# A spectral layer and a gated feed-forward: two subtractions go from GpSimd to VectorE, and their products are reordered

## The chip, the cores and the metric

The kernel runs on one core of one Trainium2 chip. The metric is the device time of one execution in microseconds (us). A core has TensorE (PE, the matrix unit; PEld is its weight load), VectorE (DVE), ScalarE (ACT), GpSimd (POOL) and SyncE (SP), which issues the DMAs here. Each engine works through its own list of instructions in order, and semaphores make one engine wait for another.

## The reference

```python
N, D, F = 8192, 448, 1792            # tokens, channels, hidden width
def _A_ref(x, w1, b1, w2, b2):       # Fourier mixing over the tokens
    Xf = rfft2(x, axes=(1, 2))
    ...                              # two complex block layers, ReLU between, soft threshold
    return irfft2(Yf, (H, W), axes=(1, 2))
def _B_ref(x, w_gate, w_up, w_down):
    return (_gelu(x @ w_gate) * (x @ w_up)) @ w_down
mod = (_silu(c) @ w_mod).reshape(1, 6, 1, -1)      # sa, ca, ga, sb, cb, gb
h = _layernorm(x) * (1 + ca) + sa
x = x + ga * _A_ref(h, A_w1, A_b1, A_w2, A_b2)
h = _layernorm(x) * (1 + cb) + sb
x = x + gb * _B_ref(h, B_w_gate, B_w_up, B_w_down)
```

## The kernel before

The first 390 us or so make the transform, the block layers and the first half of the inverse transform, whose result `vd` goes to memory. The rest works on 32 chunks of 256 tokens (`CB` = 2 tiles of 128). For a chunk it multiplies `vd` by the inverse matrix `g` (`inverse` or `winverse`), adds the residual, normalizes, and runs the feed-forward, whose hidden width is cut into 7 units (`NP`). Numbers are kept to near fp32 by splitting each into a high and a low part: `gh` and `gl` of the matrix, `vh` and `vl` of the data. `split` makes a high part by a copy on ScalarE (L115) and the low part by a subtraction on the engine given as `el` (L117). An inverse then takes three products for each tile: `gh vh`, `gl vh`, `gh vl`.

Chunks 0 to 7 (`NSTD` = 8) are the standard stage, about 390 to 775 us. For each, `gate_up` runs 14 groups k = 0 to 13 of gate and up matmuls, and after k = 2 `down` multiplies the chunk before by the down weights. `down` is a fast 2x2 scheme with seven products of 21 matmuls each (L1313 to L1315: high by high, high by low, low by high). The products share few PSUM banks: the fifth needs the one that held the third, and ScalarE's copy at L1346 empties it. Between the products, `down` calls `mid(0)`, `mid(1)` and `mid(2)`, at which other work is put into the engines' lists.

That other work is, in chunks 1 to 7, the making of the weights' *forms* for the later stage: sums and differences of gate and up weight blocks of one unit (`form_sums` parts 0, 1 and 2, at L1683, L1685 and L1688 to L1690), their cast to fp16 on ScalarE (`forms_hi`, L1719) and the low parts on VectorE (`forms_lo`, L1727). The lists `start` (chunk 1) and `steady` (chunks 2 to 7) set where each step stands. In `steady`, part 1 stands at k = 2, the form cast that reads its result (number 4) at `mid(0)`, right ahead of L1346 on ScalarE. GpSimd's list there also holds the low parts of the inverse for the chunk two ahead (`split_g`, `split_v`, put in at k = 1).

Chunks 8 to 31 are the wide stage, about 775 us to the end. It runs `period(u)` for each of 168 units: `stage_a(u)` (32 matmuls at L1496), `stage_d(u-2)` (12), `stage_c(u-1)` (22), `stage_b(u)` (10). Between stages c and d of a unit, VectorE's `joins` (L1533, L1539) read what c left in PSUM. Then come the two gelu parts on ScalarE (L1545, L1553), their multiplications on VectorE (L1549, L1556), four sums on GpSimd (L1289 to L1292), and quantization (ScalarE L1561, VectorE L1571). Once in 7 periods, at k = 2, `phase` runs `winverse` for the chunk two ahead (L1620 to L1622), its residual (L1150) and `down` of the chunk before. That chunk's data are split at k = 0 (`split_v`: ScalarE L1120, GpSimd L1123 in four pieces) and its matrix at k = 1 (`split_g`), behind that period's other work.

Of the kernel before, what the change touches and what calls it, by code (L numbers as in the profile page):

```python
# [16 lines left out]
ALU = mybir.AluOpType  # L17
# [23 lines left out]
NSTD = 8  # L41
# [9 lines left out]
def spectral_geglu(ctx, tc, x, w1, b1, w2, b2, wg, wu, wd, cvec, wmod, cf1, cs2, cmi, cgm, out):  # L51
    nc = tc.nc
    V, S, G, T = nc.vector, nc.scalar, nc.gpsimd, nc.tensor
# [59 lines left out]
    def split(hi, lo, src, eh=None, el=None):  # L113

        (eh or S.copy)(hi, src)  # L115
        h = hi.bitcast(F32) if hi.dtype == F32R else hi
        (el or V).tensor_tensor(lo, src, h, ALU.subtract)  # L117
# [26 lines left out]
    with ExitStack() as actx:  # L144
# [227 lines left out]
        pe, start = 0.0, {}  # L372
# [36 lines left out]
    with ExitStack() as bctx:  # L409
# [576 lines left out]
        draws, nxt, x1t = {}, {}, {}  # L986
# [60 lines left out]
        def split_g(i):  # L1047
            gh = ep.tile([128, CB, 128], F32R, tag="gh", name="gh")
            gl = ep.tile([128, CB, 128], F32R, tag="gl", name="gl")
            split(gh, gl, nxt[i]["g"], el=G)  # L1050
            nxt[i]["g"] = gh, gl

        def down_hi(t):
# [38 lines left out]
    with ExitStack() as cctx:  # L1092
# [523 lines left out]
        def winverse(i, ps2):  # L1616
            nxt[i]["ps"] = [ps2[:, b, 0:D] for b in range(CB)]
            (gh, gl), vh, vl = nxt[i]["g"], nxt[i]["vh"], nxt[i]["vl"]
            for b, ps in enumerate(nxt[i]["ps"]):
                T.matmul(ps, gh[:, b], vh[:, b], start=True, stop=False)  # L1620
                T.matmul(ps, gl[:, b], vh[:, b], start=False, stop=False)
                T.matmul(ps, gh[:, b], vl[:, b], start=False, stop=True)  # L1622

        def down_banks(pf):
            return lambda q: (pdn[0], pdn[1], pf[:, 0, :], pdn[0], pf[:, 1, :], pdn[1], pdn[0])[q]
# [1 line left out]
        def phase(i):  # L1627

            u = i * NP + LA
            pf = sets[(u + 1) % 3]  # L1630
            j = i + 2
            on(u - 3, quant_lo)
            if j < nch:
                winverse(j, pf)
                residual(j)
            steps = {
                0: [(stats2,), (rsqrt_part, 5)],
                1: [(rsqrt_part, 9), (norm2, 0)],
                2: [(norm2, 1)],
            }  # L1640

            def mid(n):
                for fn, *args in steps[n] if j < nch else []:
                    fn(j, *args)

            down(i - 1, down_banks(pf), mid)

        extra = {
            0: [(2, split_v)],
            1: [(2, split_g), (1, wtransposes, [0])],  # L1650
            2: [(1, wtransposes, range(1, 5))],
            3: [(2, token_sums, 0), (2, wpack_hi, [0, 1]), (2, wpack_lo, [0, 1])],
# [26 lines left out]
        def form_sums(t, part):  # L1679
            r = raws[("w", t)]  # L1680
            a11, a12, a21, a22 = (r[:, q, h : h + 3].rearrange("p c x -> p (c x)") for q in range(2) for h in (0, 3))
            if part == 0:
                G.tensor_tensor(a21, a21, a22, ALU.add)  # L1683
            elif part == 1:
                G.tensor_tensor(a11, a21, a11, ALU.subtract)  # L1685
            else:
                e1, e2 = r[:, 0, 6], r[:, 1, 6]
                G.tensor_tensor(e1, e2, e1, ALU.subtract)  # L1688
                G.tensor_tensor(a12, a12, a11, ALU.subtract)
                G.tensor_tensor(a11, a22, a11, ALU.subtract)  # L1690
# [48 lines left out]
        def store_forms(t, part):  # L1739
# [5 lines left out]
        start = [  # L1745
            (0, load_forms),
            ("m0", form_sums, 0),
            ("m0", forms_hi, 0),
            ("m1", forms_lo, 0),
            ("m1", forms_hi, 2),  # L1750
            ("m2", forms_lo, 2),
            ("m2", form_sums, 1),
            ("m2", forms_hi, 1, 3),
            (3, forms_lo, 1, 3),
            (3, forms_hi, 4),
            (4, forms_lo, 4),
            (4, form_sums, 2),
            (4, forms_hi, 5),
            (5, forms_lo, 5),
# [38 lines left out]
        for n, k in enumerate((4, 7, 11, 13)):  # L1798
# [3 lines left out]
        hooks = {  # L1802
            5: [(1, turn)],
            1: [(2, split_g), (2, split_v)],
            6: [(2, inverse)],
            7: [(2, residual)],
# [8 lines left out]
        def later_by_one(k):  # L1815
# [14 lines left out]
        soon = {  # L1830
            0: [(1, token_sums, 0), (1, token_sums, 1), (1, wpack_hi, range(3)), (1, wpack_lo, range(3))],
            1: [(1, wpack_hi, [3, 4]), (1, wpack_lo, [3, 4]), (2, split_g), (2, split_v)],
            5: [(1, turn)],
            6: [(2, inverse)],
# [137 lines left out]
        for u in range(U0, NT_ + 1):  # L1972
            period(u)
            i, k = divmod(u, NP)
# [99 lines left out]
```

## Time and profile before

| | us |
|---|---|
| median of 3 runs | 1879.49 (1878.55 to 1882.35) |
| the profiled execution | 1880.26 |
| its span, first to last instruction | 1878.5 |
| PE busy | 1818.6 (97%) |
| DVE busy | 1395.4 (74%) |
| ACT busy | 994.9 (53%) |
| POOL busy | 1330.9 (71%) |
| mean granted TensorE clock | 0.989 |

The profile is of one execution. A row of its timeline gives start and duration in us, engine, line of the kernel, operation, output <- inputs, shapes and count; a bracket gives the idle time before it and what ended that. A row of the waits says which engine and line waited for which, with the total, the number and the longest. Matrices in PSUM and SBUF carry the program's names: `pdn` are the banks of `down`, `set` the three bank sets of the wide stage, `ws` and `wr` the forms and the raw weights, `ac` the quantized activations.

### The profile page before, as it was taken

To read this page: it belongs to the slowest core of one execution; us is meant where nothing else is said; L and a number is where in the kernel's file an instruction comes from. 1 tells how busy PE (TensorE), PEld (TensorE's weight loads), DVE (VectorE), ACT (ScalarE), POOL (GpSimd) and SP (SyncE) were. 2 spreads that over 40 slices of the span, in tenths; PEclk is the share of its full clock that TensorE was granted. 3 is DMA by queue.
4 is the path that set the end of the run, shared out by engine and by line. 5 is a ranking of instruction groups with operands and counts; after the bars stand their busy time and mean duration, and the time that the engine had idled before them with its cause. 6 is when DMAs were issued, how large, how long until landed. Compare 5 with 4: busy or idle time off the path is not lost.

```text
span 1878.5 us, 55991 instructions
## 1 busy us (share of the span) xinstructions
PE 1818.6 (97%) x23040; PEld 1713.3 (91%) x23040; DVE 1395.4 (74%) x2916; ACT 994.9 (53%) x1924; POOL 1330.9 (71%) x1760
## 2 busy tenths in 40 slices
PE   7999999899999998999999999999999999999998
PEld 3698999788888887899999999999999999999998
DVE  8787999878566666777777777777777777777755
ACT  5676778544333334355555555555555555555443
POOL 3466888258677777677777777777777777777634
PEclk9999999999999999999999999999999999999999
DMA  9987778754444434966666667666666666766561
GB/s 352 332 273 248 245 197 230 209 102 103 103 104 103 89 77 102 287 175 172 178 186 174 182 181 183 175 170 170 171 170 170 175 182 176 176 183 179 151 181 56
DMA packets 386232, 332.02 MB, mean 177 GB/s; under 512 B 116404, under 2 KB 364344, under 8 KB 385976
## 3 DMA queue, kind: packets, MB, share of 16 engines
q1 hardware_dynamic: 385976, 328.45, 64.0%
q8 instruction: 180, 2.95, 0.7%
q14 instruction: 76, 0.62, 0.1%
HBM read 243.32 MB, written 60.10 MB: 162 GB/s over the span
## 4 chain that ended last, share of the span: by engine, by line
PE 41%; POOL 35%; DVE 9%; issue 6%; DMA 5%; ACT 2%; SPq 1%; POOLq 0%; ACTq 0%; DVEq 0%
POOL x L1290 6%; PE pdn L1313 5%; PE pdn L1315 5%; PE pdn L1314 5%; PE set L1496 4%; POOL x L1289 4%; PE pgu L1240 4%; POOL x L1292 4%; POOL pk L1467 3%; POOL v L1123 3%; POOL x L1328 3%; POOL cq L1327 3%; PE set L1313 2%; PE set L1315 2%; PE set L1314 2%
## 5 line engine op out<-in xcount | busy, mean ns | idle before, releaser
L1496 PE MATMUL set<-nt,wk 128*128 128x128 f16 x12768 | 717.8, 219 | 2.4 <-DMA wk<-wk 1.1
L1496 PEld LDWEIGHTS <-wk 128*128 128x128 f16 x12768 | 715.2, 98 | 2.9 <-issue 1.5
L1313 PE MATMUL pdn<-wd,ac 128*128 128x224 f16 x1218 | 318.9, 262 | 17.0 <-ACT cq L1346 17.0
L1315 PE MATMUL pdn<-wd,ac 128*128 128x224 f16 x1218 | 318.7, 262 | 0.6 <-DVE ac L1301 0.6
L1314 PE MATMUL pdn<-wd,ac 128*128 128x224 f16 x1218 | 318.7, 262 | 0.0
L1240 PE MATMUL pgu<-nt,wk 128*128 128x256 f16 (+1 forms) x2464 | 268.2, 273 | 4.6 <-DVE x L1281 4.6
L1240 PEld LDWEIGHTS <-wk 128*128 128x128 f16 (+1 forms) x2464 | 225.7, 98 | 45.8 <-issue 20.4
L1571 DVE SCALAR_TENSOR_TENSOR ac<-x,sa_act,ac 128x896 f16<-128x896 f32 x168 | 213.5, 1271 | 38.1 <-ACT ac L1561 38.1
L1289 POOL TENSOR_TENSOR x<-x 128x128 f32<-128x128 f32 x223 | 146.5, 657 | 109.2 <-DVE x L1281 61.0
L1545 ACT ACTIVATE gl<-c,dg 128x384 f32<-128x384 f32 x168 | 103.1, 613 | 216.8 <-DVE c L1539 211.8
L1290 POOL TENSOR_TENSOR x<-x 128x128 f32<-128x128 f32 x223 | 193.1, 866 | 17.5
L1561 ACT ACTIVATE ac<-x,sa_act 128x896 f16<-128x896 f32 x168 | 174.8, 1040 | 48.8 <-POOL x L1292 42.0
L1359 POOL TENSOR_TENSOR cq<-cq 128x224 f32<-128x224 f32 x32 | 21.1, 659 | 241.1 <-DVE cq L1358 241.1
L1314 PEld LDWEIGHTS <-ac 128*128 128x128 f16 x1568 | 154.7, 99 | 18.9 <-issue 18.0
L1291 POOL TENSOR_TENSOR x<-x 128x128 f32<-128x128 f32 x223 | 166.9, 748 | 0.0
L1313 PEld LDWEIGHTS <-ac 128*128 128x128 f16 x1568 | 154.7, 99 | 5.7 <-issue 4.8
L1549 DVE TENSOR_TENSOR x<-c,gl 128x384 f32<-128x384 f32 x168 | 142.9, 851 | 18.1 <-ACT gl L1545 17.1
L1315 PEld LDWEIGHTS <-ac 128*128 128x128 f16 x1568 | 154.7, 99 | 1.7 <-DVE ac L1301 0.8
L1533 DVE TENSOR_TENSOR c<-set,sb 128x512 f32<-128x512 f32 x168 | 115.3, 686 | 36.2 <-PE set L1496 34.7
L1276 ACT ACTIVATE gel<-pgu,dg 128x256 f32<-128x256 f32 x112 | 49.4, 470 | 158.7 <-PE pgu L1240 150.9
L117 POOL TENSOR_TENSOR yl<-y,yh 128x448 fp32r<-128x448 f32 x63 | 87.9, 1411 | 55.1 <-ACT yh L115 54.8
L556 DVE SCALAR_TENSOR_TENSOR y<-pm,lam,t 64x224 f32<-64x224 f32 x256 | 115.1, 449 | 10.5 <-ACT t L548 6.7
(345 smaller groups left out, 3795.4 us busy)
## 6 DMA issues: line engine op xcount, KB each, us to landing
wk<-wk SPq DMA_DIRECT2D x76, 1024.0 KB, 9.3
wk<-wk SPq DMA_DIRECT2D x76, 768.0 KB, 5.0
tr<-td SPq DMA_DIRECT2D x32, 448.0 KB, 4.7
vd<-us SPq DMA_DIRECT2D x64, 224.0 KB, 3.1
xx<-in_A_x SPq DMA_DIRECT2D x32, 448.0 KB, 4.2
v<-vd SPq DMA_DIRECT2D x63, 224.0 KB, 5.6
out<-x SPq DMA_DIRECT2D x31, 448.0 KB, 7.6
xt<-in_A_x SPq DMA_DIRECT2D x15, 896.0 KB, 14.9
```

The source lines that it names most:

```text
L1240: T.matmul(pgu[i, t, q][:, pr * H : (pr + 1) * H], ws[rows, n, w, tw], nts[i][rows, tn, :], start=start, stop=stop, skip_group_check=True,)
L1289: e.tensor_tensor(s1, a21, a22, ALU.add)
L1290: e.tensor_tensor(s2, s1, a11, ALU.subtract)
L1291: e.tensor_tensor(s3, a11, a21, ALU.subtract)
L1313: T.matmul(ps, ac[:, 0, ka], w[:, 0, kb], start=n == 0, stop=False)
L1314: T.matmul(ps, ac[:, 0, ka], w[:, 1, kb], start=False, stop=False)
L1315: T.matmul(ps, ac[:, 1, ka], w[:, 0, kb], start=False, stop=n == NP - 1)
L1496: T.matmul(ps2[:, pr, reg * 128 : reg * 128 + 128], slot[:, pr, hl, wt, :], nt[:, xt, :], start=start and j == 0, stop=j == len(terms) - 1 ...
L1533: V.tensor_tensor(c[:, :, 1:3, :], p[:, :, 0:256].rearrange("p g (r c) -> p g r c", r=2), b[:, :, 0:128].rearrange("p g (o c) -> p g o c", ...
L1549: V.tensor_tensor(xs[u][:, 1::3, :], cts.pop(u)[:, 1], gls.pop(u), ALU.mult)
L1561: S.activation(ac[:, 0], xs[u][:, 0:7], AF.Copy, scale=sa_act[:, t : t + 1])
L1571: V.scalar_tensor_tensor(ac[:, 1], xs.pop(u)[:, 0:7], sa_act[:, t : t + 1], ac[:, 0], op0=ALU.mult, op1=ALU.subtract)
```

## The change

The diff:

```diff
@@ split_g
-            split(gh, gl, nxt[i]["g"], el=G)
+            split(gh, gl, nxt[i]["g"], el=V if i > NSTD + 2 else G)
@@ winverse
                 T.matmul(ps, gh[:, b], vh[:, b], start=True, stop=False)
-                T.matmul(ps, gl[:, b], vh[:, b], start=False, stop=False)
-                T.matmul(ps, gh[:, b], vl[:, b], start=False, stop=True)
+                T.matmul(ps, gh[:, b], vl[:, b], start=False, stop=False)
+            for b, ps in enumerate(nxt[i]["ps"]):
+                T.matmul(ps, gl[:, b], vh[:, b], start=False, stop=True)
@@ form_sums
             elif part == 1:
-                G.tensor_tensor(a11, a21, a11, ALU.subtract)
+                V.tensor_tensor(a11, a21, a11, ALU.subtract)
```

`V` is VectorE and `G` GpSimd. The subtraction of part 1 is made by VectorE in all seven chunks 1 to 7. The low inverse matrix `gl` is made by VectorE for chunks 11 to 31 (`i > NSTD + 2`), 21 of them; chunk 10 and those before keep GpSimd. In all 22 calls of `winverse`, the two products with `gl` come last. Lines behind L1622 are one further down in the changed kernel: L1685 is L1686 there.

GpSimd in chunk 5, before: the forms' sum (L1683), one unit's four sums, the inverse's two low parts, and the forms' differences.

```order
L1683 TENSOR_TENSOR wr<-wr 128x384
L1289 TENSOR_TENSOR x_9274<-x_9274 128x128
L1290 TENSOR_TENSOR x_9274<-x_9274 128x128
L1291 TENSOR_TENSOR x_9274<-x_9274 128x128
L1292 TENSOR_TENSOR x_9274<-x_9274 128x128
L117 TENSOR_TENSOR gl<-g,gh 128x256
L117 TENSOR_TENSOR v<-v,vh 128x896
L1685 TENSOR_TENSOR wr<-wr 128x384
L1688 TENSOR_TENSOR wr<-wr 128x128
```

VectorE in the same place, now: the low parts of the first two forms, the subtraction, and then the first result of `down` and the third low part.

```order
L1728 SCALAR_TENSOR_TENSOR ws<-wr,sww,ws 128x3x128 x2
L1686 TENSOR_TENSOR wr<-wr 128x384
L1341 TENSOR_TENSOR cq_3433<-pdn,cq_3432 128x224
L1728 SCALAR_TENSOR_TENSOR ws<-wr,sww,ws 128x128
L1731 COPY ws<-ws 128x2x128
L1728 SCALAR_TENSOR_TENSOR ws<-wr,sww,ws 128x3x128
L1349 TENSOR_TENSOR cq_3432<-pdn,cq_3432 128x224
```

The difference has moved from behind the inverse's low parts on GpSimd to ahead of L1341 on VectorE.

VectorE ahead of the inverse of chunk 11 in the wide stage, now: the last multiplication of a unit, the low matrix, the next unit's joins, a quantization and the next multiplications.

```order
L1556 TENSOR_TENSOR x_12376<-set_11355,gl_12392 128x128
L117 TENSOR_TENSOR gl<-g,gh 128x256
L1533 TENSOR_TENSOR c<-set_11356,sb 128x2x256
L1539 TENSOR_TENSOR c<-set_11356,sb 128x2x128
L1571 SCALAR_TENSOR_TENSOR ac<-x_12273,sa_act,ac 128x896
L1549 TENSOR_TENSOR x_12479<-c,gl_12476 128x3x128
L1556 TENSOR_TENSOR x_12479<-set_11356,gl_12495 128x128
```

Before, L1533 stood right behind the first L1556, and the row with `gl<-g,gh` stood on GpSimd between two units' sums. (`gl` followed by a number is another tile, the gelu's output.)

TensorE at the inverse of the same chunk, as a difference:

```order
 L1620 MATMUL set_11356<-vh,gh 128x448
-L1621 MATMUL set_11356<-vh,gl 128x448
-L1622 MATMUL set_11356<-v,gh 128x448
+L1621 MATMUL set_11356<-v,gh 128x448
 L1620 MATMUL set_11356<-vh,gh 128x448
-L1621 MATMUL set_11356<-vh,gl 128x448
-L1622 MATMUL set_11356<-v,gh 128x448
+L1621 MATMUL set_11356<-v,gh 128x448
+L1623 MATMUL set_11356<-vh,gl 128x448 x2
```

The number of products is the same; the first one with `gl` is the fifth instead of the second.

## Prediction

> **What bounds the kernel now.** I read the waits first, then the timeline of one chunk of each stage, then the granted clock. In the rows of the waits the columns are: total us, times, longest us. The first two come from the waits of the standard stage (390 to 800 us), the third from those of the wide stage.
>
> ```profile
> PE pdn L1313 <- ACT cq L1346: 17.0, 6, 5.1
> ACT ws L1719 <- POOL wr L1685: 31.5, 6, 7.6
> PEld set L1621 <- POOL gl L117: 8.7, 21, 0.4
> 783.00:1740.00 957.00, 954.20 (x14409) 942.88 (x14408) 713.64 (x1451) 506.23 (x1008) 742.65 (x1056) 1.00 0.67 179
> ```
>
> The fourth row is the table by stretches: length, busy PE, PEld, DVE, ACT and POOL, granted clock, DMA. TensorE is busy for 954.2 of 957 us of the wide stage at clock 1.00, so there only what stops TensorE counts, and the third row names the one repeated stop with a named releaser. In the standard stage TensorE stands still six times for ScalarE's copy at L1346, and ScalarE stands still six times for GpSimd's L1685, the first difference of the weights' forms. These are one chain, as chunk 5 shows (columns: start, duration; in brackets the idle time before, and what ended it):
>
> ```profile
> 622.21 0.34 ACT L1340 COPY cq<-pdn 128x224 f32<-128x224 f32 x1 [2.08 <-PE pdn L1315]
> 622.45 0.62 ACT L1719 ACTIVATE ws<-wr,sww 128x384 f16<-128x384 f32 x1
> 627.57 0.62 ACT L1719 ACTIVATE ws<-wr,sww 128x384 f16<-128x384 f32 x1 [4.50 <-POOL wr L1685]
> 628.09 0.33 ACT L1346 COPY cq<-pdn 128x224 f32<-128x224 f32 x1
> 624.19 2.39 POOL L117 TENSOR_TENSOR v<-v,vh 128x896 fp32r<-128x896 f32 x1
> 626.54 0.99 POOL L1685 TENSOR_TENSOR wr<-wr 128x384 f32<-128x384 f32 x1
> 622.58 0.39 DVE L1341 TENSOR_TENSOR cq<-pdn,cq 128x224 f32<-128x224 f32 x1 [0.31 <-ACT cq L1340]
> 413.85 0.34 ACT L1340 COPY cq<-pdn 128x224 f32<-128x224 f32 x1 [4.52 <-PE pdn L1315]
> 416.15 0.34 ACT L1346 COPY cq<-pdn 128x224 f32<-128x224 f32 x1 [1.44 <-PE pdn L1315]
> ```
>
> GpSimd reaches L1685 only after the inverse's low part (`v`, 2.39 us). The second form cast at L1719 needs it, L1346 stands behind that cast on ScalarE, and the fifth product needs the bank that L1346 empties. The last two rows are chunk 1, whose forms are written in another order: there L1346 comes 2.30 us after L1340, when its product is done. The six stops, in full:
>
> ```profile
> 474.36 0.26 PE L1313 MATMUL pdn<-wd,ac 128*128 128x224 f16 x1 [3.69 <-ACT cq L1346]
> 526.00 0.26 PE L1313 MATMUL pdn<-wd,ac 128*128 128x224 f16 x1 [1.99 <-ACT cq L1346]
> 576.80 0.26 PE L1313 MATMUL pdn<-wd,ac 128*128 128x224 f16 x1 [2.15 <-ACT cq L1346]
> 628.46 0.26 PE L1313 MATMUL pdn<-wd,ac 128*128 128x224 f16 x1 [1.98 <-ACT cq L1346]
> 679.26 0.32 PE L1313 MATMUL pdn<-wd,ac 128*128 128x224 f16 x1 [2.14 <-ACT cq L1346]
> 733.99 0.34 PE L1313 MATMUL pdn<-wd,ac 128*128 128x224 f16 x1 [5.06 <-ACT cq L1346]
> ```
>
> Right behind four of them the granted clock (third number from the end) is 0.50; behind the other two it is not, of which 628.60 is shown:
>
> ```profile
> 474.55:477.95 3.40, 3.40 (x21) 2.76 (x20) 0.00 (x0) 0.68 (x2) 0.24 (x1) 0.50 0.02 5
> 576.95:580.35 3.40, 3.40 (x20) 2.78 (x19) 0.00 (x0) 0.71 (x2) 0.29 (x1) 0.50 0.00 0
> 628.60:632.00 3.40, 3.40 (x37) 3.40 (x36) 1.33 (x5) 0.73 (x2) 0.56 (x2) 1.00 0.00 0
> 679.30:682.70 3.40, 3.40 (x19) 2.77 (x19) 0.00 (x0) 0.82 (x2) 0.39 (x1) 0.50 0.00 0
> 733.95:737.35 3.40, 3.36 (x19) 2.65 (x19) 0.00 (x0) 0.90 (x2) 0.48 (x1) 0.50 0.02 5
> ```
>
> In 3.4 us TensorE starts 19 to 21 matmuls there, against 37.
>
> **The change, part by part. The first difference on VectorE.** It stands ahead of L1341 and needs the form's sum (L1683) and the second low part on VectorE, both there by then. Its price is bounded by the same shape with both inputs in SBUF, L1549, and lies between the minimum and the maximum:
>
> ```profile
> L1549 DVE TENSOR_TENSOR x<-c,gl x168: 546/805/1424, 779.5 to 1861.2; 128x384 f32<-128x384 f32 x168
> L1571 DVE SCALAR_TENSOR_TENSOR ac<-x,sa_act,ac x168: 1140/1215/1617, 801.6 to 1864.8; 128x896 f16<-128x896 f32 x168
> L117 DVE TENSOR_TENSOR mil<-mi,mih x1: 424/424/424, 65.8 to 65.8; 128x256 fp32r<-128x256 f32 x1
> ```
>
> I take the median, 0.81 us. In chunk 5 VectorE is free from 622.27, so it ends near 623.08; L1341 moves from 622.58 to there, 0.5 us (0.2 to 1.1 by the ends). The second cast then runs at 623.1 to 623.7, and L1346 waits for its product alone: 622.21 + 2.30 = 624.51, done by 624.85. TensorE asks for the bank at 628.46 - 1.98 = 626.48, so 1.6 us are to spare, and even 1.42 us for the difference leaves the copy on time. What VectorE does 0.5 us later (L1341, two low parts) nobody on TensorE waits for at that point. So I take all six stops away: 17.0 us. GpSimd saves 0.99 us a chunk, which hides.
>
> **The clock behind the stops.** Each of the four stretches lasts at least the 3.40 us of its row, and a stretch at half speed loses half of itself: 1.7 us each, 6.8 us for four. Without the stops I see no idle time that would call them. Ends: 0 (they come for another reason) and 6.8; all four begin at a stop's end, so 6.8.
>
> [...]
>
> **The low inverse matrix on VectorE, and its products last.** It touches chunks 11 to 31: 21 chunks, the count of the third row. With the wait, the six products take 964.49 - 962.79 = 1.70 us; in chunk 10, whose matrix was early, 782.63 - 781.29 = 1.34:
>
> ```profile
> 781.29 0.19 PEld L1620 LDWEIGHTS set<-vh,gh 128*128 128x128 f32 x1
> 782.63 0.10 PEld L1313 LDWEIGHTS <-ac 128*128 128x128 f16 x1 [0.21 <-issue]
> 962.79 0.19 PEld L1620 LDWEIGHTS set<-vh,gh 128*128 128x128 f32 x1
> 964.49 0.10 PEld L1313 LDWEIGHTS <-ac 128*128 128x128 f16 x1 [0.22 <-issue]
> 958.33 0.39 ACT L115 CAST gh<-g 128x256 fp32r<-128x256 f32 x1
> 1003.80 0.39 ACT L115 CAST gh<-g 128x256 fp32r<-128x256 f32 x1
> 957.31 2.51 POOL L1123 TENSOR_TENSOR v<-v,vh 128x224 fp32r<-128x224 f32 x4
> 958.24 0.69 DVE L1533 TENSOR_TENSOR c<-set,sb 128x512 f32<-128x512 f32 x1 [0.48 <-PE set L1496]
> 958.85 0.41 DVE L1539 TENSOR_TENSOR c<-set,sb 128x256 f32<-128x256 f32 x1
> 959.18 1.59 DVE L1571 SCALAR_TENSOR_TENSOR ac<-x,sa_act,ac 128x896 f16<-128x896 f32 x1
> 1856.49 0.41 DVE L1539 TENSOR_TENSOR c<-set,sb 128x256 f32<-128x256 f32 x1
> 1856.96 2.06 PE L1496 MATMUL set<-nt,wk 128*128 128x128 f16 x34 [0.56 <-DVE c L1539]
> L1496 PE MATMUL set<-nt,wk 128*128 128x128 f16 x12768 | 717.8, 219 | 2.4 <-DMA wk<-wk 1.1
> ```
>
> That is 0.36 us a chunk, 7.6 us in all (8.7 by the wait's own total). The reordering adds no matmul; the low inverse of `v`, asked for one matmul earlier, is done at 959.82, 3 us ahead. What GpSimd saves hides.
>
> But the subtraction now stands on VectorE ahead of the joins L1533 and L1539. It can start when ScalarE's `gh` ends, 958.72, and the joins, which began at 958.24, stand behind it. Alone it takes 0.42 (the last row of the group before), so it ends at 959.17. GpSimd is then in its four `v` pieces (957.31 to 959.82, 0.63 each). L1571, begun at 959.18 as the fourth piece began, took 1.59 instead of 1.14, as if it had started at 959.63, and not later: a VectorE operation with two SBUF inputs seems to wait out most of the one piece it meets. The third piece ends at 959.20, so the subtraction would run as if from 959.05, to 959.47. The two joins need 959.26 - 958.24 = 1.02, and at these places neighbours overlap by 0.08 (959.18 against 959.26): they end at 959.47 - 0.08 + 1.02 = 960.41. Who waits for them: the last matmuls of that unit (stage d). At 1856.96 TensorE started them 0.06 after L1539's end. They are due 44 matmuls (12 of stage d, 22 of stage c, 10 of stage b) before 962.79: at 717.8 / 12768 = 0.056 us each, 960.3 to 960.36. So each chunk gives back 960.47 - 960.36 = 0.11 us: 2.3 us, between 0 (end at 959.17) and rival one's 15.6. Net: 7.6 - 2.3 = 5.3.
>
> [...]
>
> **The sum.** 17.0 + 6.8 + 5.3 = 29.1 us, against the profiled execution (1880.26 us, span 1878.5): 1851.2. It stands 0.77 above the median of the runs, 1879.49, so the forecast is 1850.4.
>
> **The rivals.**
> *One, the joins wait out two pieces.* If the fourth `v` piece goes ahead of the subtraction, that runs as if from 959.67 and ends at 960.09; the joins end at 961.03, and stage d is 0.73 to 0.74 late, 15.6 us in 21 chunks. The wide stage then loses 8.0 and the whole gains 17.0 + 6.8 - 8.0 = 15.8: 1863.7. For it: the pieces stand back to back. Against it: L1571 met one piece and waited for that alone. Chance 0.12.
> *Two, half of the stops come back.* VectorE's later low parts, in GpSimd's way, make L1349 or L1341 the next late one. Half of 17.0 + 6.8 is 11.9: 1862.3. Against it: the 1.6 us to spare. For it: L1549's spread up to 1.42. Chance 0.12.
> *Three, slower.* One mechanism: the subtraction heads VectorE's queue and waits for ScalarE's `gh`, behind a quantization that itself waits for GpSimd. VectorE may lose about 1.0 us there unseen (960.36 - 0.06 - 959.26 = 1.04); each further us costs 21. Without the joins the gain is 29.1 + 2.3 = 31.4 (1848.1); with the 3.8 that a measurement tells, 35.2 us are needed: joins 1.04 + 35.2 / 21 = 2.7 us late, to come out slower: `gh` ending near 960.6 rather than 958.72. At 3 us late: 1848.1 + 21 x 1.96 = 1889. Nothing on the trace points to it; chance 0.04.
> *Four, stretches at half clock stay.* If the two behind the short stops (2.15 and 2.14 us) are not made by them, two remain: 1850.4 + 3.4 = 1853.8; if none of the four is, 1857.2. Against it: each begins where a stop ends. Chance 0.08. [...]
> *Five, no change:* something unseen takes the place of both waits. 1879.5, chance 0.03.
>
> **How the numbers follow.** The forecast as worked out keeps 0.61, with a range of its own from 1847 (no joins' loss, the wait's 8.7: 17.0 + 6.8 + 8.7 = 32.5) to 1855. The range goes over rivals four, two and one, to 1864; below, 1846. A measurement here tells about 0.2%, 3.8 us, from no change: faster 0.93, same 0.03, slower 0.04.
>
> **What would show it.** Right: no row of TensorE waiting for L1346; clock 1.00 through 466 to 750 us; the third wait gone; six inverse products in 1.34 us; a chunk of the wide stage 0.25 us shorter than 45.47 (1003.80 - 958.33). Wrong: TensorE waiting for L1539 by more than 0.2 us a chunk (rival one), or for L1349 or L1341 in chunks 2 to 7 (rival two), or 0.50 rows without a stop (rival four).

## The result, and the profile after

| | before | after |
|---|---|---|
| median, us | 1879.02 (1877.32 to 1882.35, 4 runs) | 1852.03 (1851.05 to 1853.30, 4 runs) |
| the profiled execution, its span | 1880.26, 1878.5 | 1853.30, 1851.4 |
| mean granted TensorE clock | 0.989 | 0.992 |

The ratio is 0.9855, 95% interval 0.9837 to 0.9872: 27.0 us faster by the medians, 27.1 by the spans, against a forecast of 29.1 (1850.4). The sum came out 2 us high: it held no term for the change of stage, which cost 2.0 us, nor for the first 415 us, where 1.3 us went and where no part of the change was expected to act; and two of its terms were 1.4 us low.

First the waits of the standard stage (390 to 800 us; columns: total, times, longest). These are the first three rows of TensorE there, and ScalarE's longest wait for the forms:

```profile
PE pgu L1240 <- DVE x L1281: 4.1, 6, 1.2
PE set L1496 <- ACT sb L1524: 2.5, 1, 2.5
PE pdn L1315 <- DVE ac L1301: 0.6, 1, 0.6
ACT ws L1720 <- POOL wr L1689: 19.3, 7, 5.4
```

The row for L1346 (17.0 us) is gone. ScalarE still waits 19.3 us for GpSimd, now for the next form (L1689), but that cast stands behind the copy at L1346, and nobody on TensorE waits for it. The second row, at the change of stage, is the one that grew: it was 0.7 us before. Chunk 5 after, from the timeline:

```profile
611.92 0.35 ACT L1340 COPY cq<-pdn 128x224 f32<-128x224 f32 x1 [2.08 <-PE pdn L1315]
614.22 0.35 ACT L1346 COPY cq<-pdn 128x224 f32<-128x224 f32 x1 [0.84 <-PE pdn L1315]
612.09 0.64 DVE L1686 TENSOR_TENSOR wr<-wr 128x384 f32<-128x384 f32 x1
612.65 0.38 DVE L1341 TENSOR_TENSOR cq<-pdn,cq 128x224 f32<-128x224 f32 x1
614.25 2.40 POOL L117 TENSOR_TENSOR v<-v,vh 128x896 fp32r<-128x896 f32 x1
```

The difference (L1686) took 0.64 us on VectorE, and L1346 starts 2.30 us after L1340, when its product is done, as in chunk 1 of before. The low part of `v` starts only then, at 614.25, and runs to 616.65: nothing that TensorE needs here stands behind it any more.

The distance from one chunk's L1340 to the next is what a chunk costs. Rows of before, then of after:

```profile
467.04 0.34 ACT L1340 COPY cq<-pdn 128x224 f32<-128x224 f32 x1
519.74 0.35 ACT L1340 COPY cq<-pdn 128x224 f32<-128x224 f32 x1 [2.08 <-PE pdn L1315]
570.38 0.34 ACT L1340 COPY cq<-pdn 128x224 f32<-128x224 f32 x1 [1.62 <-PE pdn L1315]
```

```profile
468.38 0.34 ACT L1340 COPY cq<-pdn 128x224 f32<-128x224 f32 x1
515.59 0.35 ACT L1340 COPY cq<-pdn 128x224 f32<-128x224 f32 x1 [2.07 <-PE pdn L1315]
564.08 0.35 ACT L1340 COPY cq<-pdn 128x224 f32<-128x224 f32 x1 [1.60 <-PE pdn L1315]
```

The first of these distances fell from 52.70 to 47.21 us, by 5.49: the stop of 3.69 and 1.80 more for the half-clock stretch behind it. The second fell from 50.64 to 48.49, by 2.15: the stop of 1.99 and 0.16 more, without a half-clock stretch. The next three fell by 3.99, 2.15 and 3.96, and the last stretch, to the first L1496, by 6.84 (stops of 2.15, 1.98, 2.14, 5.06).

The wide stage, at the place of the chunk that the prediction used (ScalarE's `gh`, VectorE's list, GpSimd's pieces, and the weight loads that begin the six products and follow them):

```profile
936.53 0.39 ACT L115 CAST gh<-g 128x256 fp32r<-128x256 f32 x1
981.71 0.39 ACT L115 CAST gh<-g 128x256 fp32r<-128x256 f32 x1
936.96 0.74 DVE L117 TENSOR_TENSOR gl<-g,gh 128x256 fp32r<-128x256 f32 x1 [1.00 <-ACT gh L115]
937.62 0.68 DVE L1533 TENSOR_TENSOR c<-set,sb 128x512 f32<-128x512 f32 x1
938.22 0.41 DVE L1539 TENSOR_TENSOR c<-set,sb 128x256 f32<-128x256 f32 x1
935.51 2.70 POOL L1123 TENSOR_TENSOR v<-v,vh 128x224 fp32r<-128x224 f32 x4
941.08 0.19 PEld L1620 LDWEIGHTS set<-vh,gh 128*128 128x128 f32 x1
942.40 0.10 PEld L1313 LDWEIGHTS <-ac 128*128 128x128 f16 x1 [0.22 <-issue]
```

A chunk takes 45.18 us instead of 45.47, and the six products 1.32 instead of 1.70. The subtraction ran beside the pieces and took 0.74 us, as in all 21 chunks (0.42 in the row at 65.8 us that the prediction took); it ended 0.78 us after `gh` (936.92 to 937.70), where the prediction had 0.75 (958.72 to 959.47). L1539 ends at 938.63, and the matmul 44 ahead of the inverse starts at 938.68, 0.16 us after the one before it instead of the usual 0.056.

The change of stage is the first L1496 to the first L1620. The rows are the table by stretches (length, busy PE, PEld, DVE, ACT, POOL, granted clock, DMA) and TensorE's timeline, of before and then of after, there with ScalarE's cast:

```profile
768.85:781.29 12.44, 10.63 (x183) 10.22 (x181) 10.58 (x17) 8.90 (x21) 12.27 (x19) 1.00 1.09 346
773.87 1.95 PE L1496 MATMUL set<-nt,wk 128*128 128x128 f16 x32 [0.66 <-ACT sb L1524]
776.96 4.55 PE L1496 MATMUL set<-nt,wk 128*128 128x128 f16 x76 [1.15 <-DMA wk<-wk]
```

```profile
745.61:760.07 14.46, 11.97 (x183) 11.81 (x181) 9.81 (x17) 8.98 (x21) 12.46 (x20) 0.88 1.10 344
752.47 7.82 PE L1496 MATMUL set<-nt,wk 128*128 128x128 f16 x108 [2.49 <-ACT sb L1524]
751.00 0.94 ACT L1120 CAST vh<-v 128x896 fp32r<-128x896 f32 x1 [2.81 <-DMA v<-vd]
```

It got 2.02 us longer. ScalarE waits 2.81 us for the load of `vd` (0.97 before), the copy at L1524 stands behind that cast, TensorE waits 2.49 us for the copy, and part of the rest runs at half clock (0.88 over the stretch). The wait for the weights' load that followed before, 1.15 us, is not there after.

By spans: up to chunk 1's L1340, 1.3 us lost (413.85 to 415.16), from there to the change of stage 24.6 gained, 2.0 lost at it, and 5.9 gained behind it (1097.2 to 1091.3): 27.1 in all.

### The profile page after: what moved, and what is told of

It reads as the page before. It is cut to its first block, busy times and chain, and to the rows that moved or that the text cites. A ratio compares the mean times of both kernels' runs of the same rounds, so it can differ in the third digit from the quotient of the medians.

```text
span 1851.4 us, 55998 instructions
## 1 busy us (share of the span) xinstructions
PE 1807.8 (98%) x23040; PEld 1710.9 (92%) x23040; DVE 1404.3 (76%) x2944; ACT 991.2 (54%) x1924; POOL 1316.2 (71%) x1732
## 4 chain that ended last, share of the span: by engine, by line
PE 85%; DVE 6%; DMA 2%; POOL 2%; ACT 2%; SPq 1%; issue 1%; ACTq 0%; DVEq 0%; POOLq 0%
PE set L1496 37%; PE pgu L1240 11%; PE pdn L1313 6%; PE pdn L1315 6%; PE pdn L1314 6%; PE ps L213 2%; PE set L1313 2%; PE set L1314 2%; PE set L1315 2%; DVE y L556 1%; DVE hl L486 1%; DVE st L174 1%; PE set L1620 1%; PE pm L539 1%; PE pm L511 1%
## 5 line engine op out<-in xcount | busy, mean ns | idle before, releaser
L1496 PE MATMUL set<-nt,wk 128*128 128x128 f16 x12768 | 721.2, 219 | 3.2 <-ACT sb L1524 2.5
L1496 PEld LDWEIGHTS <-wk 128*128 128x128 f16 x12768 | 717.6, 98 | 4.8 <-issue 3.6
L1315 PE MATMUL pdn<-wd,ac 128*128 128x224 f16 x1218 | 315.5, 259 | 0.6 <-DVE ac L1301 0.6
L1313 PE MATMUL pdn<-wd,ac 128*128 128x224 f16 x1218 | 315.7, 259 | 0.0
L1314 PE MATMUL pdn<-wd,ac 128*128 128x224 f16 x1218 | 315.5, 259 | 0.0
L1571 DVE SCALAR_TENSOR_TENSOR ac<-x,sa_act,ac 128x896 f16<-128x896 f32 x168 | 205.0, 1220 | 35.8 <-ACT ac L1561 35.7
L1289 POOL TENSOR_TENSOR x<-x 128x128 f32<-128x128 f32 x223 | 129.5, 581 | 108.3 <-DVE x L1281 59.4
L1290 POOL TENSOR_TENSOR x<-x 128x128 f32<-128x128 f32 x223 | 185.3, 831 | 17.5
L1291 POOL TENSOR_TENSOR x<-x 128x128 f32<-128x128 f32 x223 | 173.1, 776 | 0.0
L1292 POOL TENSOR_TENSOR x<-x 128x128 f32<-128x128 f32 x223 | 139.5, 626 | 0.0
L1533 DVE TENSOR_TENSOR c<-set,sb 128x512 f32<-128x512 f32 x168 | 115.0, 685 | 26.8 <-PE set L1496 25.3
L117 POOL TENSOR_TENSOR yl<-y,yh 128x448 fp32r<-128x448 f32 x63 | 88.2, 1417 | 54.6 <-ACT yh L115 54.3
```

Of the source, the lines that this page charges most:

```text
L1289: e.tensor_tensor(s1, a21, a22, ALU.add)
L1290: e.tensor_tensor(s2, s1, a11, ALU.subtract)
L1291: e.tensor_tensor(s3, a11, a21, ALU.subtract)
L1292: e.tensor_tensor(s4, a12, s2, ALU.subtract)
L1313: T.matmul(ps, ac[:, 0, ka], w[:, 0, kb], start=n == 0, stop=False)
L1314: T.matmul(ps, ac[:, 0, ka], w[:, 1, kb], start=False, stop=False)
```

## The experiments

All against the kernel before, whose medians were 1879.98 beside the first four and 1880.23 beside the last three.

**Only the forms' difference on VectorE.**

```diff
-                G.tensor_tensor(a11, a21, a11, ALU.subtract)
+                V.tensor_tensor(a11, a21, a11, ALU.subtract)
```

> Only the forms' first difference goes to VectorE; the low inverse matrix and the order of its products stay as before. Theory (the two parts add, each in its own stage): all six stops at L1346 and the four half-clock stretches behind them go (17.0 + 6.8 us), the change of stage gives back about 2.0 us as in the changed kernel, the wide stage keeps 45.47 us a chunk and its 21 waits of 0.4 us: about 22 us faster than before, 1857. Rival (the stages are tied, the wide stage's gain hangs on GpSimd being freed earlier too): a chunk of the wide stage gets shorter than 45.47 by at least 0.1 us without any change there, and the time comes out below 1854.

Measured: 1858.5 us, ratio 0.9889 (0.9876 to 0.9901). The six stops are gone, and no stretch at half clock is left between 390 and 800 us. That the stops came from L1685 alone holds. Two other parts of the theory do not. The change of stage gave back 0.3 us (12.77 against 12.44), not 2.0. And the wide stage, whose code is that of before, does not stay as it was: its chunks alternate.

```profile
841.25 0.39 ACT L115 CAST gh<-g 128x256 fp32r<-128x256 f32 x1
886.99 0.39 ACT L115 CAST gh<-g 128x256 fp32r<-128x256 f32 x1
932.59 0.39 ACT L115 CAST gh<-g 128x256 fp32r<-128x256 f32 x1
885.96 3.37 POOL L1123 TENSOR_TENSOR v<-v,vh 128x224 fp32r<-128x224 f32 x4
931.57 2.53 POOL L1123 TENSOR_TENSOR v<-v,vh 128x224 fp32r<-128x224 f32 x4
PEld set L1621 <- POOL gl L117: 13.0, 21, 0.8
```

The distances are 45.74 and 45.60, and so on to the end, against 45.47 before. Ahead of one `gh` GpSimd's four `v` pieces take 3.37 us, ahead of the next 2.53 (2.51 before), and the wait for `gl` grows from 8.7 to 13.0 us. Twenty chunks of 0.2 us are 4 us of the gain given back. That the time still came out near the forecast of 1857 is luck: by spans 2.2 us were gained ahead of chunk 1's L1340 (413.85 to 411.60), 24.6 from there to the change of stage, and 0.3 and 4.4 were lost at it and behind it.

The change of stage deserves a second look, because up to it this kernel and the changed one execute the same instructions. This is its cast:

```profile
746.08 0.94 ACT L1120 CAST vh<-v 128x896 fp32r<-128x896 f32 x1 [1.48 <-DMA v<-vd]
```

ScalarE waits 1.48 us for `vd` where it waited 2.81, TensorE 1.16 us for L1524 where it waited 2.49, and no half clock follows. The load was issued 5.6 us ahead of the first L1496 here (736.45 and 742.02), and 4.7 ahead in the changed kernel (740.91 and 745.61). In SyncE's list five transposes (L1480) stand ahead of it; together they took 7.7 us here and 8.8 there. So the 2.0 us are the price in one execution.

**Only the order of the six products**, with GpSimd's `gl`:

```diff
-                T.matmul(ps, gl[:, b], vh[:, b], start=False, stop=False)
-                T.matmul(ps, gh[:, b], vl[:, b], start=False, stop=True)
+                T.matmul(ps, gh[:, b], vl[:, b], start=False, stop=False)
+            for b, ps in enumerate(nxt[i]["ps"]):
+                T.matmul(ps, gl[:, b], vh[:, b], start=False, stop=True)
```

> Only the six inverse products are reordered, with those of the low matrix last; GpSimd still makes it. Theory (the order alone takes the wait away): the low matrix was 0.40 us late for the second product; as the fifth it is asked for 3 products of 0.2 us later, so the wait is gone, nothing is added on VectorE, and a chunk takes 45.47 - 0.38 = 45.09 us: about 8 us faster, 1871. The six stops and the half-clock stretches of the standard stage stay. Rival (VectorE's faster subtraction is what matters): GpSimd is still late for the fifth product, at least 0.2 us a chunk stays, and the gain is under 4 us.

**Only `gl` on VectorE**, the old order kept:

```diff
-            split(gh, gl, nxt[i]["g"], el=G)
+            split(gh, gl, nxt[i]["g"], el=V if i > NSTD + 2 else G)
```

> Only the low inverse matrix of chunks 11 to 31 goes to VectorE; the products keep their order. Theory (order and engine each take the whole wait away, VectorE pays for it with the joins): a chunk takes 45.18 us, as in the changed kernel, 6 us faster in all, 1873, and the joins end about 0.4 us later than before against the inverse. Rival (both are needed): the second product still waits, a chunk takes 45.3 us or more.

Measured: 1872.1 us (0.9956, 0.9941 to 0.9971) and 1873.7 us (0.9971, 0.9960 to 0.9982). Two neighbouring `gh` rows of the first, then of the second:

```profile
960.99 0.39 ACT L115 CAST gh<-g 128x256 fp32r<-128x256 f32 x1
1006.07 0.39 ACT L115 CAST gh<-g 128x256 fp32r<-128x256 f32 x1
```

```profile
957.26 0.39 ACT L115 CAST gh<-g 128x256 fp32r<-128x256 f32 x1
1002.43 0.39 ACT L115 CAST gh<-g 128x256 fp32r<-128x256 f32 x1
```

45.08 and 45.17 us: either edit alone takes the whole wait for `gl` away, and neither trace has a row of it. Their difference is 0.09 to 0.10 us a chunk (the second's distances are 45.17 and 45.18), and it lies where the prediction put it, at the joins. In the second, the matmul 44 ahead of each inverse starts 0.05 us after L1539's end and 0.15 after the matmul before it; in the first, 1.12 and 0.056. So the order alone takes the wait away, and VectorE's part costs about 2 us in 21 chunks between these two kernels.

Both kernels keep the six stops, 17.0 us. But the half-clock stretches behind them do not stand where they stood before. From the first of the two kernels, the stretch at its second stop and the one at its third:

```profile
529.49 0.26 PE L1313 MATMUL pdn<-wd,ac 128*128 128x224 f16 x1 [1.99 <-ACT cq L1346]
530.20:533.60 3.40, 3.40 (x22) 2.81 (x20) 0.32 (x2) 0.15 (x1) 0.00 (x0) 0.55 0.00 0
581.95 0.26 PE L1313 MATMUL pdn<-wd,ac 128*128 128x224 f16 x1 [2.15 <-ACT cq L1346]
581.00:584.40 3.40, 2.45 (x26) 2.44 (x26) 0.24 (x1) 1.76 (x4) 1.39 (x3) 1.00 0.00 0
```

The shorter stop, 1.99 us, is followed by half clock here and the longer, 2.15, is not; before it was the other way round. The last section comes back to this.

**The forms on VectorE and the new order, without VectorE's `gl`** (the first two edits together):

> The forms' difference on VectorE and the reordered products, but the low inverse matrix stays on GpSimd in all chunks. Theory (VectorE's subtraction ahead of the joins costs 0.09 us a chunk and brings nothing that the order doesn't): a chunk takes 45.09 us instead of 45.18, and the time is 1.5 to 2 us below the changed kernel, 1850. Rival (the subtraction on GpSimd pushes its sums and so the quantization back): a chunk takes 45.18 us or more, the time is that of the changed kernel or above, 1852 to 1855.

Measured: 1850.68 us, 0.9841 (0.9828 to 0.9853): 1.4 us under the changed kernel by medians taken beside different runs of before. By the spans it is 2.5 us (1848.9 against 1851.4), but all 2.5 are there already at chunk 1's L1340 (412.70 against 415.16), ahead of everything in which the two kernels differ. So leaving out VectorE's `gl` is not shown to gain or lose here, and that the time is the theory's is luck. Neither forecast of the chunk came. The wide stage alternates too, 45.01 and 45.32, mean 45.16, with part of the wait for `gl` back:

```profile
PEld set L1623 <- POOL gl L117: 3.0, 11, 0.3
```

**The place in the list, not the engine.** Here no work changes its engine; the inverse's low parts, and ScalarE's high copies with them, stand at k = 3 instead of k = 1, behind the forms:

```diff
-            1: [(2, split_g), (2, split_v)],
+            3: [(2, split_g), (2, split_v)],
...
-            1: [(1, wpack_hi, [3, 4]), (1, wpack_lo, [3, 4]), (2, split_g), (2, split_v)],
+            1: [(1, wpack_hi, [3, 4]), (1, wpack_lo, [3, 4])],
+            3: [(2, split_g), (2, split_v)],
```

> The kernel before, with no work moved to another engine: only the place of the inverse's two low parts (and their high copies) in the lists of the standard stage moves, from k = 1 to k = 3, so that GpSimd comes to L1685 right behind the forms' sums. My theory is that the six stops came from the place in GpSimd's list, not from GpSimd being slow: then no TensorE row waits for L1346, the half-clock stretches behind the stops go, and the standard stage gains what it gained in the changed kernel, 24.6 us, less about 2 us at the change of stage; the wide stage keeps its wait for L117 and its 45.47 us a chunk (or the 45.67 of the run with only the forms on VectorE): 1857 to 1861. The rival is that VectorE's speed is needed: GpSimd's subtraction (0.99 us against about 0.5) keeps the second form cast behind the third product, at least 1 us of each stop stays, and the time is 1866 or more.

Measured: 1862.72 us, 0.991 (0.9891 to 0.9929), between the two forecasts. In chunk 5 GpSimd now makes the difference in time. L1346 still stands behind the cast and starts some 0.5 us after its product is done (by the 2.30 us of above: 609.81, the start of L1340, + 2.30 = 612.11), but TensorE no longer waits for it:

```profile
611.11 0.99 POOL L1685 TENSOR_TENSOR wr<-wr 128x384 f32<-128x384 f32 x1
612.14 0.61 ACT L1719 ACTIVATE ws<-wr,sww 128x384 f16<-128x384 f32 x1 [1.47 <-POOL wr L1685]
612.66 0.33 ACT L1346 COPY cq<-pdn 128x224 f32<-128x224 f32 x1
630.33 0.47 PE L1141 MATMUL pi<-v,gh 128*128 128x448 f32 x1 [0.42 <-POOL v L117]
PE pdn L1313 <- ACT cq L1346: 3.3, 2, 2.4
PE pi L1141 <- POOL v L117: 2.1, 5, 0.4
```

Four of the six stops are gone without VectorE, so the place in GpSimd's list made them. Two stay, 0.98 us in chunk 2 and 2.35 in chunk 7: in chunk 7 three other GpSimd operations (L1467, from 710.09 on) stand ahead of L1685 (712.22) even then, and a half-clock stretch follows that stop. And the low part moved back is itself late: the inverse waits for it in five chunks, 0.4 us on TensorE, and those from the third form chunk on are 0.7 us longer than in the changed kernel (49.2 and 48.5 against 48.5 and 47.9). So the place was the cause of those four stops, and VectorE the better cure, since it leaves the low part where it was.

**An earlier load.** In chunk 7 the load of `vd` for chunk 10 is issued at k = 6 instead of k = 9, ahead of a store of forms and a load of weights. First on top of the kernel with the forms and the order, then on top of the changed kernel:

```diff
-                    load_v(i + 3)
+                    if i < NSTD - 1:
+                        load_v(i + 3)
...
+                if (i, k) == (NSTD - 1, 6):
+                    load_v(i + 3)
```

> The kernel with the forms' difference on VectorE and the products reordered (1850.7 us), in which the load of vd for chunk 10 is issued three groups earlier in chunk 7, ahead of a store of forms and a load of weights. My theory of the 2 us lost at the change of stage: ScalarE's cast at L1120 waits for that load, L1524 stands behind it, TensorE waits 2.5 to 2.7 us for L1524, and a stretch at half clock follows. Then without the late load TensorE's wait for L1524 falls under 1 us, the half-clock stretch near 751 us goes, and the time falls by 2 to 4 us, to 1846.5 to 1848.5. The rival is that the DMAs there are late together: the weights' load takes the place of the wait, at least 2 us of it stay, and the time stays within 1 us of 1850.7.

> The changed kernel whole, with the same earlier load of vd for chunk 10 and nothing else. By my theory it falls by 2 to 4 us, to 1848 to 1850, with a wide stage of 45.18 us a chunk as in the changed kernel. By the rival (another DMA takes its place) it stays at 1851.5 to 1852.5. If the phase in which VectorE and GpSimd enter the wide stage matters more than either, the chunk's 45.18 itself moves, by up to 0.3 us, 7 us over the wide stage in either direction.

Measured: 1847.1 us (0.9823, 0.9803 to 0.9842) and 1847.75 us (0.9831, 0.9812 to 0.9850); the first is the lowest median of this study, though the two intervals overlap. The change of stage in the second, with its cast at L1120 and TensorE's one wait:

```profile
742.55:755.01 12.46, 10.53 (x183) 10.19 (x181) 10.72 (x17) 9.16 (x21) 12.29 (x19) 1.00 1.09 345
745.02 0.94 ACT L1120 CAST vh<-v 128x896 fp32r<-128x896 f32 x1
750.80 4.43 PE L1496 MATMUL set<-nt,wk 128*128 128x128 f16 x76 [1.82 <-DMA wk<-wk]
```

The cast no longer waits, the wait for L1524 is gone, the clock stays at 1.00, and the change of stage takes 12.46 us, as before the change (12.44) and 2.00 less than after it. The rival was right in part: 1.82 us of waiting for the weights' load take the place of 2.49, about as much as the two waits of before (0.66 and 1.15). The span fell by 5.4 us, but 2.9 of them lie ahead of chunk 1's L1340 (415.16 to 412.25), where nothing was edited; 2.0 lie at the change of stage. Over all nine traces its length follows ScalarE's wait for `vd`: 12.44 to 12.47 us with a wait of 1.0 or less, 12.74 and 12.77 with 1.3 and 1.5, 14.46 and 15.10 with 2.8 and 3.1. In the first kernel the change of stage fell from 15.10 (without the earlier load) to 12.47, and its wide stage, whose code was not touched, no longer alternates:

```profile
796.99 0.39 ACT L115 CAST gh<-g 128x256 fp32r<-128x256 f32 x1
842.08 0.39 ACT L115 CAST gh<-g 128x256 fp32r<-128x256 f32 x1
887.15 0.39 ACT L115 CAST gh<-g 128x256 fp32r<-128x256 f32 x1
```

45.09 and 45.07 instead of 45.01 and 45.32: 2 us over the stage. The time at which the engines enter the loop may decide which of the two it settles in; with one trace of each kernel, this isn't shown.

## Why the prediction was right, and where its sum was off

*The stops, 17.0.* Right, and by the mechanism given: no L1346 row is left, and the change's first edit alone removes all six. The difference took 0.64 us where 0.81 was taken, and both were far within the 1.6 us to spare. Rival two did not come.

*The clock, 6.8.* The four stretches went. The chunk distances fell by 24.6 us, of which 17.0 are the stops; of the 7.6 left, 7.2 lie behind the four stops with a stretch, 1.8 each, and 0.3 behind the two without. The size was 0.8 low. The reason given was incomplete: behind the stops of 1.98 and 1.99 us in this trace, and behind the one of 2.15 us with the order alone, there is no half clock (below). The four stretches of this trace went with their stops; but the stops alone did not settle that there were four: with the same six the kernel with the order alone had five, 17.1 us, and the one with VectorE's `gl` alone six, 20.5. The runs without a trace point the same way: eleven executions of the kernel before, beside the last three experiments, go from 1874.42 us with a granted clock of 0.993 to 1884.10 with 0.987.

*The wide stage, 5.3.* Measured 5.9. Without the joins' price a chunk saves 45.47 - 45.08 = 0.39 us (0.36 was taken), and the joins take back 0.09 to 0.10 (0.11). Rival one did not come: the subtraction ended 0.78 us after `gh`, where rival one had 1.37 (958.72 to 960.09). That VectorE waits out most of a piece was the prediction's estimate from the one row of L1571. The traces show the times: in the one of before, L1571 starts within 0.03 us of the start of the fourth piece in 21 chunks and takes 1.59 to 1.62 us each time; after, it starts 0.33 to 0.34 us behind the pieces and takes 1.14. What happens between the two engines meanwhile they do not show. The joins' mechanism is shown: stage d starts 0.05 us after L1539's end in the traces with VectorE's `gl`, where the prediction had 0.06, and 1.12 after it with the order alone. What the prediction did not see is that the new order alone suffices for the wait.

*The change of stage, not in the sum: -2.0.* This is the step that failed. What would be late next, once the stops were gone, was asked inside the chunks only. TensorE came to it 23.2 us earlier, the issue of the load of `vd` 21.9 us (762.76 to 740.91), and the first stop that remained was a cast waiting for `vd` with TensorE's copy behind it. The two kernels with the earlier load, and the nine traces side by side, show that it was this load. Its size is that of one execution: the same instructions cost 0.3 us with the forms alone and 2.7 with the forms and the order.

*The first 415 us: -1.3.* Nearly all of the code there is the same in all kernels, so this is most likely the difference between two executions. Over the nine profiled executions chunk 1's L1340 stands between 409.83 and 417.35 us. A difference of two profiled spans can therefore be off by several us; the distances inside a stage, and the medians, tell more.

29.1 + 0.8 + 0.6 - 2.0 - 1.3 = 27.2, against 27.1 by the spans. That the forecast came within 2 us of the median is in part luck, since errors of both signs stand in this sum.

## What to carry to other kernels

When an engine waits for a small operation, look at what stands ahead of that operation in its engine's list: here it stood behind one of 2.39 us, and moving it to VectorE's list took away six stops, 17.0 us. Either of two edits alone took away the third wait, 8.7 us, so the one without a price should be tried first. When a stage gets faster, follow the DMAs that the next stage starts with: here the load was issued 21.9 us earlier and TensorE came 23.2 us earlier. In a loop on which several engines work, measure the distance between iterations, and two in a row: here they were 45.01 and 45.32 us in one kernel and 45.08 in another with the same loop.

## What the runs showed of the hardware

*The stretches at half clock stand on a grid in each run.* The stretches in the trace of before start at 474.52, 576.92, 679.32 and 733.93 us, and each is 3.41 us long. The starts are 102.4, 102.4 and 54.6 us apart: 30, 30 and 16 steps of 3.413 us. In each of the nine traces all stretches of the run, from the first at 22 to 155 us to the last near the end, start on one such grid, to 0.01 of a step. If each stop of TensorE of 0.5 us or more between 390 and 800 us is cut at the grid of its run, the part that fell into one step and the clock of the next went together like this:

| idle in one step of the grid, us | cases | next step |
|---|---|---|
| 1.98 to 3.41 | 17 | half clock, in all |
| up to 1.82 | all others, the longest 1.40, 1.46, 1.50, 1.58, 1.64, 1.70, 1.82 | full clock, but for the one of 1.50 |

The one of 1.50 us lay in a step that was at half clock already. So behind a stop of 1.98 to 2.15 us there was a stretch (1.84 and 1.82 us more than the stop itself, in the chunk distances of before) or none (0.16 and 0.17), by where on the grid it fell, and behind the same six stops stood 13.7 us of half clock before, 17.1 with the reordering alone and 20.5 with VectorE's `gl` alone. No case lies between 1.82 and 1.98 us, and the ends of matmuls are modelled in these records, so the table says no more than its rows, and for 390 to 800 us only. Elsewhere in the trace of before half clock also follows steps with 1.71 us of idle time (102.47 to 105.88) and 1.63 (242.41 to 245.82); and in five of the nine traces it follows, near 75 us, a step in which TensorE's records show no idle time of more than 0.01 us (71.75 to 75.16 in the trace of before). What sets the clock there was not shown.

*The same loop took equal times or two by turns.* With one and the same code of the loop, the wide stage took 45.01 and 45.32 us by turns, or 45.08 in every chunk, and of the code ahead of it only the place of one load differed. With the code of before it took 45.47 or 45.49, or 45.60 and 45.74 by turns. In the chunks of the last kind GpSimd's four `v` pieces take 3.37 and 2.53 us by turns. Each of these is one trace; what leads to the one or the other was not tried.
